# Reordering the weight differences and sums between the first and second group of a fused attention and maxout kernel

## The chip, the cores and the metric

The kernel runs on one core of one Trainium2 chip. The metric is the device time in microseconds. Of the kernel before, three runs gave 413.27 to 413.98 us, with a median of 413.74 us. In the profile, PE is the matrix engine (TensorE), DVE is VectorE, ACT is ScalarE, POOL is GpSimd, and SP is SyncE, which here issues nearly all transfers.

## The reference

Two blocks follow each other. The first is a gated linear attention, run over 768 tokens for 4 batches of 8 heads with a head dimension of 48:

```python
f = 1.0 / (1.0 + np.exp(-f_logit))
for t in range(S):
    state = f[:, :, t, :, None] * state + np.einsum('bhd,bhe->bhde', k[:, :, t], v[:, :, t])
    y[:, :, t] = np.einsum('bhd,bhde->bhe', q[:, :, t], state)
```

The result is laid out as 3072 tokens of 384 features and goes through a maxout layer. The three input weights are 384 x 768, the output weight is 768 x 384:

```python
h = np.maximum(np.maximum(x @ w1, x @ w2), x @ w3)
return (h @ w_out).astype(np.float32)
```

## The kernel before

The attention is cut into 24 units. A unit is a chunk of 64 tokens of two batches, all heads, so 128 rows. Four units make a group of 512 tokens, and the maxout layer runs on a group when its attention is complete. There are six groups, 0 to 5.

For a unit u, `sigmoids(u)` makes the gates on ScalarE and `scan(u)` their running products on VectorE. `after(u)` turns k on VectorE (L296, `kt`), multiplies it on GpSimd (L340, `kh`) and copies the ends (L339). `before(u)` makes the other running product (L347), turns q (L296, `qt`) and multiplies it on GpSimd (L351, `qh`). `carry(u)` scales the state (L357). On TensorE, `values`, `sums`, `pairs` and `finish` are the four blocks of 32 small products (L415, L433, L396, L504) that stand together once per unit. `keys_by_blocks` makes the transposes `ks` on VectorE (L382). ScalarE copies a finished unit into the token tile `xT` (L511), and two transfers (`pack`, L524) move parts of it to other partitions: one pair for the first three units of a group, and one pair for the last.

The maxout layer rewrites the maximum as differences: w2 and w3 have w1 subtracted, and the part with w1 becomes one linear product. Group 0 computes its maxima directly in `ffn_first`, while the weights arrive and are rounded. For the groups after it, `inputs_by_pairs` computes products of two token halves with fewer multiplications, in the manner of Strassen. It needs sums and differences of the weights, made once by `mix_in(0)` to `mix_in(3)` (L850): `w_sum[0]` for the step `fifth`, `w_sum[1]` for `sixth`, a difference written in place for `seventh` and `w_sum[2]` for `third`. The sums of tokens t1 to t5 come from `sums_of_x` (L865), and `join` (L899) adds two partial results; both are on GpSimd. The maxima are finished on VectorE (L924, L931, L932).

`outputs_by_pairs` multiplies the maxima by the output weights in the same manner, for all groups. It is a generator: each step issues some products (L629) and then yields its cost. Three PSUM banks a, b and c are in use. In group 0 its 24 steps, counted from 0, are:

- 0 to 7: plain products into b and a, after which ScalarE reads a (`read(a, 0)`, L634) and VectorE adds b (L637)
- 8 and 9: s1 into c, with a copy of c to `tops` on ScalarE (L683 or L685)
- 10 and 11: s2 into a, with `read(a, 1)`
- 12 to 15: products with the third difference and the linear part into a, with `read(a, 2)`, and then a sum of outputs on GpSimd (L697)
- 16 and 17: the linear part into c
- 18 and 19: products with the fourth difference into a, and the issue of the next group's `sums_of_x` when its tokens are there
- 20 and 21: the linear part with `lin_mix`, which is `w_mix[4]`, into a; a copy to the output on ScalarE (L714)
- 22 and 23: s4 into c, and a sum of outputs on VectorE

The flag `tight` puts s2 (steps 10 and 11) ahead of s1 (steps 8 and 9). Before the change it holds in the last two groups only.

The differences of output weights are made by `mix(0)` to `mix(4)` (L577); `mix(4)` writes `w_mix[4]`. In group 0, the list `made` says what is issued after which step: the sums of maxima s1 and s2 (L593) after steps 0 to 2, s4 after step 9, `mix_in(0)` to `mix_in(3)` after steps 10 to 13, and `mix(4)` after step 14. All these are on GpSimd.

The order is written out by hand. The main loop runs over the units u from 4 on (unit n = u + 1 is prepared while u is multiplied) and calls `fill(ns)` between its parts. `fill` draws steps from the pending maxout generators until their costs have used up a budget. Every engine works through its own queue in this order. SyncE's queue has, around unit 8, the moves of weights (`place`, L458 and L465), the pack transfers, and the loads of f, k and q (L183, eight transfers for a pair of units each) and v (L164). A load of q, or of k, for units 10 and 11 is issued in unit 8; those of units 12 and 13 in unit 9.

Of the kernel before, what the change touches and what calls it, by code (L numbers as in the profile page):

```python
# [55 lines left out]
def kernel(  # L56
# [12 lines left out]
    nc = tc.nc  # L69
    B, H, S, D = q.shape  # L70
    HP = H // 2
    NU = B // 2 * (S // C)
# [5 lines left out]
    GRP = 4  # L78
# [11 lines left out]
    def fast():  # L90
        ctx = ExitStack()
        with ctx:
# [511 lines left out]
            def outputs_by_pairs(g, hm, xT):  # L604
                tile_of = lambda p, n: slice((2 * p + n) * UT, (2 * p + n + 1) * UT)
                half = lambda n: slice(n * HD, (n + 1) * HD)
                mixed = g > 0
# [13 lines left out]
                    lin_mix = [w_mix[4][:, k] for k in range(NK)]  # L621
                    partial = [rests[:, 0], rests[:, 1], rests[:, 0]]
                last = g == NU // GRP - 1
                tight = g >= NU // GRP - 2
                begun = set()

                def into(b, p, lhs, rhs, part=slice(None)):
# [165 lines left out]
            def ffn_first(xT):  # L793
                hm = new_hm()
                steps = [(j, slice(n * HALF, (n + 1) * HALF)) for n in range(2) for j in range(J_HALF)]
                steps += [(j, slice(0, TOK)) for j in range(J_HALF, NJ)]
                n_step = 0
                for j, t in steps:
                    w = t.stop - t.start
                    for i in (1, 2):  # L800
                        p = yield from product(xT, j, i, t)
                        if i == 1:
                            nc.scalar.copy(hm[:, j, t], p)
                        else:
                            nc.vector.scalar_tensor_tensor(hm[:, j, t], hm[:, j, t], 0.0, p, op0=ALU.max, op1=ALU.max)
                        round_to(ROUNDED[n_step])
                        load_weights(2, rounded[0] - 1)
                        yield (1 if w == TOK else NK) * w * COLUMN
                        n_step += 1
                        if n_step in TURNED:  # L810
                            yield from turn(TURNED[n_step])
                for n in range(2 * NK + 2):
                    place(placed[0].bitcast(FP32), w_in[1], n)
                for a in range(NK):
                    for n, cost in enumerate(linear(a)):
                        round_to(rounded[0] + 1)
                        if a == 0 and n:
                            mix(n - 1)
                        if a == 0 and n == NK - 1:
                            mix(n)  # L820
                        yield cost
                for dst, src in ((placed[1].bitcast(FP32), w_in[2]), (w_lin, w_nat)):
                    for n in range(2 * NK + 2):
                        place(dst, src, n)
                mix(3)
                made = [[lambda jj=jj: sums_of_hm(hm, jj, slice(0, 2))] for jj in range(HJ)]
                made[-1] += [lambda jj=jj: sums_of_hm(hm, jj, slice(2, 3)) for jj in range(HJ)]
                made += [[], [], [], [], [], []]
                made += [[lambda jj=jj: sums_of_hm(hm, jj, slice(3, 4)) for jj in range(HJ)]]
                made += [[lambda n=n: mix_in(n)] for n in range(4)] + [[lambda: mix(4)]]  # L830
                made = iter(made)
                for cost in outputs_by_pairs(0, hm, xT):
                    for make in next(made, ()):
                        make()
                    yield cost
# [5 lines left out]
            w_two = [t.bitcast(FP32) for t in placed[0:2]]  # L841
            w_sum = [w_in[2][:, n] for n in range(NK)]

            def mix_in(n):

                dst, x, y, op = ((w_sum[0], w_two[1][:, 0], w_two[1][:, 1], ALU.add),
                                 (w_sum[1], w_sum[0], w_two[0][:, 0], ALU.subtract),
                                 (w_two[1][:, 0], w_two[0][:, 0], w_two[1][:, 0], ALU.subtract),
                                 (w_sum[2], w_two[0][:, 1], w_sum[1], ALU.subtract))[n]
                nc.gpsimd.tensor_tensor(dst, x, y, op=op)  # L850

            packed, summed = {}, {}
            halves = lambda xT, k, h: xT[:, k, h * HALF:(h + 1) * HALF]
# [15 lines left out]
            def inputs_by_pairs(g, hm, xT):  # L869
                X = lambda k, h: halves(xT, k, h)  # L870
                t1, t2, t3, t4, t5 = sums_of_x(g)
                s1, s2, s4 = w_sum
                s3 = w_two[1][:, 0]
                COST = 2 * HALF * COLUMN
                out = lambda n, h: hm[:, 2 * n:2 * n + 2, h * HALF:(h + 1) * HALF]
                first, u3 = rests[:, 0:2, 0:HALF], tops[:, 2:4, 0:HALF]
                A, B, U5 = {}, {}, {}

                def into(b, n, w, x, begin=False):
                    for j in range(2):  # L880
                        nc.tensor.matmul(b[:, j * HALF:(j + 1) * HALF], lhsT=w[:, (2 * n + j) * 128:(2 * n + j + 1) * 128],  # L881
                                         rhs=x, start=begin and j == 0, stop=True, skip_group_check=True)

                def plain(n):
                    B[n] = bank(True)
                    into(B[n], n, w_two[0][:, 1], X(1, 0), True)
                    yield COST
                    into(B[n], n, w_two[0][:, 2], X(2, 0))
                    nc.scalar.copy(out(n, 0), two(B[n]))  # L889
                    yield COST  # L890

                def start(n):
                    A[n] = bank()
                    into(A[n], n, w_two[0][:, 0], X(0, 0), True)
                    nc.scalar.copy(first, two(A[n]))
                    yield COST

                def join(n):
                    nc.gpsimd.tensor_tensor(out(n, 0), out(n, 0), first, op=ALU.add)  # L899

                def fifth(n):
                    into(B[n], n, s1, t1, True)
                    U5[n] = two(new_top(TOK))
                    nc.scalar.copy(U5[n], two(B[n]))
                    yield COST

                def sixth(n):
                    into(A[n], n, s2, t2)
                    nc.scalar.copy(out(n, 1), two(A[n]))
                    yield COST  # L910

                def seventh(n):
                    into(A[n], n, s3, t3)
                    yield COST
                    into(A[n], n, w_two[1][:, 2], X(2, 1))
                    nc.scalar.copy(u3, two(A[n]))
                    nc.gpsimd.tensor_tensor(u3, u3, U5[n], op=ALU.add)
                    yield COST

                def third(n):  # L920
                    into(B[n], n, s4, X(1, 1))
                    yield COST
                    into(B[n], n, w_two[0][:, 2], X(2, 1))
                    nc.vector.tensor_tensor(out(n, 1), two(B[n]), out(n, 1), op=ALU.add)  # L924
                    yield COST

                def fourth(n):
                    into(A[n], n, w_two[1][:, 1], t4)
                    yield COST
                    into(A[n], n, w_two[1][:, 2], t5)  # L930
                    nc.vector.scalar_tensor_tensor(out(n, 0), out(n, 0), 0.0, two(A[n]), op0=ALU.max, op1=ALU.max)  # L931
                    nc.vector.scalar_tensor_tensor(out(n, 1), out(n, 1), 0.0, u3, op0=ALU.max, op1=ALU.max)  # L932
                    sums_of_hm(hm, n)
                    if g == 1:
                        for i in ((0, 1), (2, 3, 4), ())[n]:
                            mix_x(i)
                    yield COST

                yield from start(0)
                yield from plain(0)  # L940
                join(0)
                if g > 1:
                    store_late()
                yield from plain(1)
                yield from sixth(0)
                yield from fifth(0)
                for n in range(1, NJ // 2):
                    if n > 1:
                        yield from plain(n)
                    yield from seventh(n - 1)  # L950
                    yield from start(n)
                    join(n)
                    yield from third(n - 1)
                    yield from fifth(n)
                    yield from sixth(n)
                    yield from fourth(n - 1)
                    store_late()
                yield from seventh(NJ // 2 - 1)
                yield from third(NJ // 2 - 1)
                yield from fourth(NJ // 2 - 1)  # L960
# [35 lines left out]
            with tc.manual_schedule():  # L996
# [78 lines left out]
                for u in range(GRP, NU):  # L1075
                    n = u + 1
# [38 lines left out]
                    if n < NU:  # L1115
                        after(n)
                        before(n)
                    check_range(u - CHECKS, 0)
                    fill(part)
                    if BY_ROWS < u + 2 < NU and u % GRP == 0:  # L1120
# [292 lines left out]
```

## Time and profile before

| what | value |
|---|---|
| median of three runs | 413.74 us (413.27 to 413.98) |
| the profiled execution | 414.71 us |
| its span in the profile | 413.0 us |
| mean granted TensorE clock | 0.992 |
| TensorE busy (products) | 392.8 us, 95% |
| VectorE busy | 296.5 us, 72% |
| GpSimd busy | 257.5 us, 62% |
| ScalarE busy | 181.3 us, 44% |
| bytes moved by transfers | 47.21 MB |

Times in the views are microseconds from the start of the span. A row of a timeline gives the start, the duration, the engine, the line, the operation, the tiles written and read with their shape, and how many instructions are merged. In brackets stands the idle time before it and what ended it. A row of the waits names who waited for whom, the total, the number of times and the longest.

### The profile page before, as it was taken

The page shows a single profiled execution, that of the slowest core. Times are in us where ns is not written, and L with a number is a line of the kernel's source. Part 1 is how long each engine was busy: PE and PEld are TensorE (multiplying, and loading weights), DVE is VectorE, ACT ScalarE, POOL GpSimd, SP SyncE. Part 2 cuts the span into 40 slices and gives each one's busy share as a digit, 9 for nine tenths or more (in the row PEclk, how much of TensorE's full clock was granted, in tenths as well). Part 3 has the DMA queues.
Part 4 walks back from the last instruction along what each step waited for, and adds up shares of the span by engine and source line. Part 5 has one row for each costly group of instructions (what it writes and reads, how often), then busy time and mean ns, then how long its engine had stood idle before and what let it go on. Part 6 is the DMA issues. An engine that isn't in the chain of part 4 may idle for free.

```text
span 413.0 us, 11671 instructions
## 1 busy us (share of the span) xinstructions
PE 392.8 (95%) x4658; PEld 341.9 (83%) x4658; DVE 296.5 (72%) x571; ACT 181.3 (44%) x431; POOL 257.5 (62%) x284
## 2 busy tenths in 40 slices
PE   4988999999959999999999999999999999999995
PEld 3766765559858889998889998889988889988995
DVE  5997797999947799899799898898985650001600
ACT  2477787423204352335442435442344424487220
POOL 2179595789994777747685487496287860435700
PEclk9999999999969999999999999999999999999999
DMA  8988986768356775367664277645374002452002
GB/s 165 238 250 223 307 234 80 155 88 138 87 95 89 109 151 112 80 85 111 97 155 73 59 116 95 115 116 104 50 141 124 2 17 83 115 153 76 2 19 62
DMA packets 181594, 47.21 MB, mean 114 GB/s; under 512 B 160480, under 2 KB 179232, under 8 KB 181536
## 3 DMA queue, kind: packets, MB, share of 16 engines
q1 hardware_dynamic: 178048, 45.62, 54.0%
q10 hardware_dynamic: 3488, 0.81, 0.9%
q8 instruction: 37, 0.61, 0.6%
q14 instruction: 21, 0.17, 0.1%
HBM read 37.75 MB, written 4.72 MB: 103 GB/s over the span
## 4 chain that ended last, share of the span: by engine, by line
PE 79%; SPq 7%; POOL 5%; DMA 2%; DVE 2%; issue 2%; ACT 2%; POOLq 0%
PE p L881 19%; PE p L629 16%; PE tr L881 15%; PE tr L629 12%; PE p L542 6%; PE y L415 3%; SPq L183 3%; PE a L396 2%; SPq L174 2%; PE y L504 2%; PE a L433 2%; DMA raw<-in_moe_w_dram 2%; POOL w_in L850 1%; SPq L164 1%; POOL w_in L752 1%
## 5 line engine op out<-in xcount | busy, mean ns | idle before, releaser
L382 DVE STREAM_TRANSPOSE ks<-kh 32x128 f32<-32x128 f32 x256 | 77.4, 302 | 14.9 <-POOL kh L340 10.7
L881 PE MATMUL tr<-xT,placed 128*128 128x256 f32 x180 | 44.4, 384 | 0.0
L339 POOL COPY ends<-r 128x8 f32<-128x8 f32 x24 | 7.9, 328 | 50.0 <-DVE r L329 50.0
L329 DVE TENSOR_TENSOR_SCAN r<-gate,from_one 128x520 f32<-128x520 f32 x24 | 33.2, 1384 | 6.4 <-issue 3.0
L881 PEld LDWEIGHTS tr<-xT,placed 128*128 128x128 f32 x180 | 33.5, 190 | 4.9
L340 POOL TENSOR_TENSOR kh<-kt,r 128x512 f32<-128x512 f32 x18 | 31.9, 1771 | 8.5 <-DVE kt L296 8.5
L542 PE MATMUL p<-xT,w_in 128*128 128x256 f32 (+1 forms) x108 | 33.9, 458 | 3.3 <-POOL w_in L752 2.2
L593 POOL TENSOR_TENSOR w_in<-hm 128x256 f32<-128x256 f32 x18 | 13.3, 739 | 33.5 <-DVE hm L932 33.5
L511 ACT COPY xT<-y 64x256 f32<-64x256 f32 (+1 forms) x60 | 22.1, 369 | 22.7 <-PE y L504 22.0
L347 DVE TENSOR_TENSOR_SCAN prod<-gate,from_inv 128x520 f32<-128x520 f32 x24 | 31.6, 1317 | 0.0
L881 PE MATMUL tr<-xT,w_in 128*128 128x256 f32 x120 | 30.8, 379 | 0.0
L629 PE MATMUL p<-placed,hm 128*128 128x192 f32 x144 | 29.8, 333 | 0.7 <-POOL kh L340 0.7
L881 PE MATMUL p<-w_in,placed 128*128 128x256 f32 x120 | 30.4, 382 | 0.0
L637 DVE TENSOR_TENSOR o<-tr,w_in 128x384 f32<-128x384 f32 (+1 forms) x11 | 5.7, 521 | 33.4 <-PE tr L629 29.0
L542 PEld LDWEIGHTS p<-xT,w_in 128*128 128x128 f32 x108 | 19.5, 190 | 12.3 <-issue 6.0
L881 PE MATMUL p<-xT,placed 128*128 128x256 f32 x120 | 29.2, 379 | 0.0
L629 PE MATMUL tr<-w_out,w_in 128*128 128x192 f32 x144 | 29.0, 329 | 0.0
L924 DVE TENSOR_TENSOR hm<-tr,hm 128x512 f32<-128x512 f32 x15 | 10.2, 683 | 23.1 <-PE tr L881 16.2
L258 POOL TENSOR_TENSOR w_in<-top_bits,rest_bits 128x384 uint32<-128x384 uint32 x18 | 21.4, 1197 | 7.6 <-DVE top_bits L252 4.7
L881 PEld LDWEIGHTS p<-w_in,placed 128*128 128x128 f32 x120 | 22.4, 190 | 4.4 <-issue 1.6
L629 PEld LDWEIGHTS p<-placed,hm 128*128 128x128 f32 x144 | 23.8, 190 | 2.3 <-ACT w_in L634 1.1
L899 POOL TENSOR_TENSOR hm<-hm,rest_bits 128x512 f32<-128x512 f32 x15 | 19.1, 1272 | 10.2 <-ACT hm L889 10.2
(168 smaller groups left out, 989.9 us busy)
## 6 DMA issues: line engine op xcount, KB each, us to landing
raw<-in_moe_w_dram SPq DMA_DIRECT2D x24, 384.0 KB, 4.4
v_ld<-in_v_dram SPq DMA_DIRECT2D x48, 96.0 KB, 3.3
placed<-in_moe_w_dram SPq DMA_DIRECT2D x12, 384.0 KB, 5.9
out_dram<-o SPq DMA_DIRECT2D x45, 96.0 KB, 2.2
placed<-in_moe_w_out_dram SPq DMA_DIRECT2D x6, 384.0 KB, 6.2
f_ld<-in_f_logit_dram SPq DMA_DIRECT2D x36, 64.0 KB, 2.7
k_ld<-in_k_dram SPq DMA_DIRECT2D x36, 64.0 KB, 2.6
q_ld<-in_q_dram SPq DMA_DIRECT2D x36, 64.0 KB, 2.8
```

The source lines that it names most:

```text
L183: nc.sync.dma_start(out=blocks[nm][u // 2 % 2][p0:p0 + 32, n, :, 0:w], in_=src[:, par::2, t0 + n * 32:t0 + (n + 1) * 32, e0:e0 + w].rearrange(
L258: nc.gpsimd.tensor_tensor(dst, by(top), by(rest), op=ALU.add)
L329: nc.vector.tensor_tensor_scan(r[:, 0:LEN][:, ::-1], flat(gate)[:, ::-1], flat(from_one)[:, ::-1], 1.0, op0=ALU.mult, op1=ALU.max)
L340: (nc.vector if u < BY_ROWS else nc.gpsimd).tensor_tensor(kh.rearrange("p h a t -> p a h t"), kt, by_batch(r[:, 1:LEN + 1].rearrange("p (x ...
L347: nc.vector.tensor_tensor_scan(flat(prod), flat(gate_tiles[u % 2]), flat(from_inv[u % 2]), 1.0, op0=ALU.mult, op1=ALU.max)
L382: nc.vector.transpose(ks[n * 32:(n + 1) * 32, :, par, e0:e0 + 32], kh[p0:p0 + 32, :, a, t0:t0 + 32])
L511: nc.scalar.copy(xT[o, :, t0 + a * C:t0 + (a + 1) * C], y[i, a, 0:HP * C].rearrange("p (h t) -> p h t", h=HP))
L542: nc.tensor.matmul(p if w < TOK else p.rearrange("p (two t) -> p two t", two=2), lhsT=w_in[i][:, kt, j * 128:(j + 1) * 128], rhs=x[:, t.st ...
L593: engine.tensor_tensor(dst, x, y, op=op)
L629: nc.tensor.matmul(b[:, p * HD:(p + 1) * HD], lhsT=x, rhs=w, start=id(b) not in begun, stop=True, skip_group_check=True)
L881: nc.tensor.matmul(b[:, j * HALF:(j + 1) * HALF], lhsT=w[:, (2 * n + j) * 128:(2 * n + j + 1) * 128], rhs=x, start=begin and j == 0, stop= ...
L899: nc.gpsimd.tensor_tensor(out(n, 0), out(n, 0), first, op=ALU.add)
```

## The change

In group 0, the flag `tight` now holds as well, so the s2 products come ahead of the s1 products. `mix(4)` is issued after step 10, and `mix_in(0)` and `mix_in(1)` after steps 11 and 12. `mix_in(2)` moves to VectorE, behind `before(9)` in unit 8 of the main loop. `mix_in(3)` stays on GpSimd and is issued at the beginning of the second group's input products, behind its `sums_of_x`.

```diff
-                tight = g >= NU // GRP - 2
+                tight = not mixed or g >= NU // GRP - 2
...
                 made += [[lambda jj=jj: sums_of_hm(hm, jj, slice(3, 4)) for jj in range(HJ)]]
-                made += [[lambda n=n: mix_in(n)] for n in range(4)] + [[lambda: mix(4)]]
+                made += [[lambda: mix(4)]] + [[lambda n=n: mix_in(n)] for n in range(2)]
                 made = iter(made)
...
-            def mix_in(n):
+            def mix_in(n, engine=nc.gpsimd):
 
                 dst, x, y, op = ((w_sum[0], w_two[1][:, 0], w_two[1][:, 1], ALU.add),
                                  (w_sum[1], w_sum[0], w_two[0][:, 0], ALU.subtract),
                                  (w_two[1][:, 0], w_two[0][:, 0], w_two[1][:, 0], ALU.subtract),
                                  (w_sum[2], w_two[0][:, 1], w_sum[1], ALU.subtract))[n]
-                nc.gpsimd.tensor_tensor(dst, x, y, op=op)
+                engine.tensor_tensor(dst, x, y, op=op)
...
+                if g == 1:
+                    mix_in(3)
                 yield from start(0)
                 yield from plain(0)
                 join(0)
...
                     if n < NU:
                         after(n)
                         before(n)
+                    if u == 2 * GRP:
+                        mix_in(2, nc.vector)
                     check_range(u - CHECKS, 0)
                     fill(part)
```

## The prediction

> **What bounds the kernel now.** I read the chain that ended last first: after 126 us it is almost wholly TensorE, and before that it runs through GpSimd's weight differences at L850 and L577. So I asked which waits TensorE has between 90 and 126 us (us in total, times, longest):
>
> ```profile
> PE p L629 <- POOL placed L577: 4.2, 1, 4.2
> PE p L629 <- POOL kh L340: 0.7, 1, 0.7
> ```
>
> The timelines of GpSimd and of TensorE (start, us, engine, line) show the first wait from both sides.
>
> ```profile
> 106.67 2.11 POOL L593 TENSOR_TENSOR w_in<-hm,w_in 128x256 f32<-128x256 f32 x3
> 108.73 1.82 POOL L850 TENSOR_TENSOR w_in<-placed 128x768 f32<-128x768 f32 x1
> 110.63 1.82 POOL L850 TENSOR_TENSOR w_in<-w_in,placed 128x768 f32<-128x768 f32 x1
> 112.41 2.75 POOL L850 TENSOR_TENSOR placed<-placed,placed 128x768 f32<-128x768 f32 x1
> 115.12 2.73 POOL L850 TENSOR_TENSOR w_in<-placed,w_in 128x768 f32<-128x768 f32 x1
> 117.82 1.39 POOL L577 TENSOR_TENSOR placed<-w_in 128x576 f32<-128x576 f32 x1
> ```
>
> ```profile
> 112.95 2.11 PE L629 MATMUL p<-placed,hm 128*128 128x192 f32 x12
> 119.26 4.21 PE L629 MATMUL p<-placed,xT 128*128 128x192 f32 x12 [4.20 <-POOL placed L577]
> 123.26 2.46 PE L629 MATMUL tr<-w_out,w_in 128*128 128x192 f32 x12
> ```
>
> Four mix_in sums (9.1 us) stand in GpSimd's queue ahead of mix(4), which TensorE needs next. It idles 4.20 us, and then 24 matmuls take from 119.26 to 125.72 where 24 at the usual pace (1.95 per 12, start to start) take 3.9. The view by windows has a granted clock of 0.65 from 119.3 to 126.0 and 1.00 on both sides. The price is 4.2 + 2.6 us.
>
> SyncE decides what becomes of it. From 84 to 149 us it issues transfers back to back:
>
> ```profile
> 119.43 1.30 SPq L524 DMA_DIRECT2D xT<-xT  x2
> 122.28 4.29 SPq L183 DMA_DIRECT2D k_ld<-in_k_dram  x8
> 126.70 5.14 SPq L183 DMA_DIRECT2D q_ld<-in_q_dram  x8
> 132.42 4.83 SPq L183 DMA_DIRECT2D f_ld<-in_f_logit_dram  x8
> 137.35 5.26 SPq L183 DMA_DIRECT2D k_ld<-in_k_dram  x8
> ```
>
> The last q transfer (issued 131.42) took this to land, by the view of that tile:
>
> ```profile
> DMA to landing us min/median/max: 3.1/3.1/3.1
> ```
>
> So q of units 10 and 11 is there at 134.5. VectorE turns it at 135.86, only 1.3 us later, and then works almost without a break until TensorE needs its maxima (VectorE, then TensorE):
>
> ```profile
> 135.86 0.68 DVE L296 STREAM_TRANSPOSE qt<-q_ld 128x512 f32<-128x512 f32 x1
> 164.57 0.69 DVE L932 SCALAR_TENSOR_TENSOR hm<-hm,top_bits 128x512 f32<-128x512 f32 x1
> ```
>
> ```profile
> 165.30 0.81 PE L629 MATMUL p<-w_out,hm 128*128 128x192 f32 x4
> ```
>
> **The Trainium skill.** "TensorE: Matmul & The Clock Gate", What's actually happening, says that an idle window of about 3.4 us halves the array's clock and that a similar busy time restores it. The trace agrees: 4.20 us of idling cost 2.6 us more, the 0.7 us wait nothing. "SBUF — State Buffer", Who interferes with whom, says that GpSimd and VectorE exclude each other on a shared port pair when VectorE has two SBUF inputs and GpSimd reads SBUF. The trace agrees in kind: a 128x768 sum took 1.82 us, and 2.75 beside VectorE's scans. The end of a transfer I take from the trace, 2.4 to 3.1 us.
>
> **The change, part by part.**
>
> mix(4) behind the s4 sums, ahead of mix_in: it starts at 108.73 and takes 1.39, so it is done at 110.1. TensorE reaches step 20 (lin_mix) at 115.06 by the rows above. The wait goes, and with it the slow clock: 4.2 + 2.6 = 6.8 us.
>
> s2 ahead of s1 (`tight`): the 0.66 us wait at 104.82 was for read(a, 1) on ScalarE (104.20 + 0.48). The s1 products now stand between, so it goes. In exchange s2 needs read(a, 0), which ended at 100.18; TensorE wanted to go on at 100.10 and starts at about 100.3. Net gain 0.4. Together 7.2: TensorE begins group 1 at 118.4 instead of 125.56. Its first products need only the first copy into xT (L524, issued 111.51 to 113.56), not the second (landed about 122.2).
>
> mix_in(0) and (1) follow mix(4): 110.1 to 112.0 and to 113.8, or 114.7 beside the scan. Then the output sum (1.0), ends, kh(9), qh(9) at about 118.5, state at 119.3. kh(9) came at 120.26 before, so this is no delay. The five x sums wait for the second copy, 122.3 to 126.0, where they started at 123.3 before.
>
> mix_in(3) behind them on GpSimd: 1.82 to 2.75, done by 127.8 to 128.8. third(0) is the eleventh step of group 1: 118.4 + 10 x 0.865 (a step of four 128x256 rows, 2.59 for three in the chain) + 2.1 of attention between (127.3 to 129.4) = 129.2. Hidden with 0.4 us to spare. join(0) behind it ends at 129.2 to 130; its next reader on ScalarE (L895) wants it at 136.74 - 7.2 = 129.5. If the cover is gone, up to 1 us of TensorE.
>
> mix_in(2) on VectorE: not seen there at this size. The nearest row, 128x384 at L752, took 0.55 to 1.36; twice that is 1.1 to 2.7, and I take 1.1. It stands behind qt(9), which ended at 116.86, where VectorE idled 4.62 us for kh(9). Queued behind it are the transposes of kh(9), which may now start at 117.3 and start at 118. TensorE needs them a unit later. Cost nothing; without cover 1.1 to 2.7. It issues no transfer, and no SyncE instruction moves.
>
> **Where the 7.2 us stop.** SyncE's order and pace don't hang on TensorE here: its queue is full from 84 us. So q(10) still lands at 134.5, but TensorE would come to pairs(10) at 142.73 - 7.2 = 135.5. VectorE turns q from 134.57 to 135.25, GpSimd's qh takes 1.18, so pairs(10) starts at 136.5: 1.0 us of a new wait. Worse, VectorE stood waiting for q with its other work queued behind. From qt(10) to the end of L932 in the third pair it took 165.26 - 135.86 = 29.4 us, of which it idled 0.42 + 0.28 + 1.48 + 0.34 = 2.5. Compressed, with 0.2 given back to a sum on GpSimd at L917, that is 27.1 us: 134.57 + 27.1 = 161.7. TensorE's second half of the 165.30 group (at 165.62) then starts at 161.7, and its gain is 3.9 us. It waits some 2 us there, too short to slow the clock. Behind it the sums at L593 and qh(12) move 3.6 us with VectorE (qh(12) at 168.6, pairs(12) at 169.0), so no more is lost. From 175 on SyncE waits for TensorE again (its xT copies), and the rest moves as one.
>
> Sum against the profiled execution: span 413.0 - 3.9 = 409.1; device time 414.71 - 3.9 = 410.8. That execution stands 0.97 above the median 413.74, so I predict 413.74 - 3.9 = 409.8.
>
> **Rivals.**
>
> Loads don't bind, all is kept: 413.74 - 7.2 = 406.5. For: one of q's issues took 1.36 us where its neighbours took 0.49, so the landing may come 0.9 sooner. Against: it would have to come 3.3 us sooner, at 131.2, when SyncE is still issuing it. Chance 0.13.
>
> The new 2 us wait at 159 to 161.7 slows the clock as the old one did: 3.9 - 2.6 = 1.3, so 412.4. For: it falls together with short waits for the first half of the maxima. Against: 0.7 us did not, and 2 is under the stated window. Chance 0.08.
>
> Slower: the compressed VectorE stretch from 134.6 collides with GpSimd more often. Each collision costs about 0.9 us (2.03 against 1.18 for kh at L340; 2.75 against 1.82 at L850). It decides from five more on: 3.9 - 5 x 0.9 = -0.6; six give 415.2. For: nearly every VectorE operation there has two inputs. Against: the order on both queues is the same, and both move together. Chance 0.06.
>
> No change: mix(4) waits for something else. Its inputs, the linear products, were copied out at 92.5, and what it overwrites was free before; or the q loads fall 3 us further behind. 413.7, chance 0.05.
>
> **How the numbers follow.** The forecast has 0.68, with a range of its own of 408.6 to 411.0: 0.9 sooner for q's landing, 1.2 later for a collision and mix_in(3) coming late. 407.0 to 412.6 holds it, the clock case and the edge of the full gain, about 8 in 10. 0.2% (0.8 us) is about what a measurement of this kernel can tell from no change. Faster 0.68 + 0.13 + 0.08 = 0.89, same 0.05, slower 0.06.
>
> **What would show it.** Right: no wait of lin_mix's products for L577, clock 1.00 from 115 to 126, group 1's first products at 118 to 119, a wait of VectorE before qt(10) ending at 134 to 135, waits of TensorE at pairs(10) (about 1 us) and at the last hm rows of group 1 (about 2), and the shift constant from 170 on. Wrong: q landing sooner with TensorE unbroken, or TensorE waiting for L850 at third(0), or a clock below 1 after 130.

## The result and the profile after

The changed kernel takes 408.62 us (median of 4 runs, 406.68 to 410.12), the kernel before 413.50 us beside it. The ratio is 0.9878, with a 95% interval of 0.9833 to 0.9923: 4.9 us faster, between 3.2 and 6.9. The forecast was 409.8.

The profiled execution took 408.11 us, with a span of 406.4 us. The page has a granted clock of 9 tenths or more in all forty slices; before, one slice had 6. The same stretch of TensorE's timeline as before (start, us, engine, line) now reads:

```profile
111.04 2.11 PE L629 MATMUL p<-placed,hm 128*128 128x192 f32 x12
112.99 2.12 PE L629 MATMUL p<-placed,xT 128*128 128x192 f32 x12
114.94 2.11 PE L629 MATMUL tr<-w_out,w_in 128*128 128x192 f32 x12
116.89 1.03 PE L881 MATMUL p<-xT,placed 128*128 128x256 f32 x4
```

Steps 18 to 23 of group 0 follow each other without a gap, at 1.95 us per twelve. GpSimd has mix(4) ahead of two sums, and the third sum is on VectorE:

```profile
107.46 1.42 POOL L577 TENSOR_TENSOR placed<-w_in 128x576 f32<-128x576 f32 x1
108.82 1.82 POOL L850 TENSOR_TENSOR w_in<-placed 128x768 f32<-128x768 f32 x1
110.73 2.72 POOL L850 TENSOR_TENSOR w_in<-w_in,placed 128x768 f32<-128x768 f32 x1
```

```profile
115.08 1.10 DVE L850 TENSOR_TENSOR placed<-placed,placed 128x768 f32<-128x768 f32 x1
130.16 0.71 DVE L296 STREAM_TRANSPOSE qt<-q_ld 128x512 f32<-128x512 f32 x1 [0.95 <-DMA q_ld<-in_q_dram]
```

The second row is the turn of q(10). VectorE now waits for the load, 0.95 us, which it did not do before. It comes late with the maxima, and TensorE waits for them once:

```profile
157.41 1.19 PE L629 MATMUL p<-w_out,hm 128*128 128x192 f32 x4 [0.61 <-DVE hm L931]
```

Where the time went is seen from the block of 32 small products at L415, which TensorE runs once per unit. These are its starts in the two timelines:

| L415 block | before | after | difference |
|---|---|---|---|
| unit 6 | 93.11 | 91.85 | -1.3 |
| unit 7 | 105.97 | 104.06 | -1.9 |
| unit 8 | 127.38 | 118.71 | -8.7 |
| unit 9 | 141.76 | 133.10 | -8.7 |
| unit 10 | 156.91 | 148.25 | -8.7 |
| unit 11 | 171.89 | 164.38 | -7.5 |
| span | 413.0 | 406.4 | -6.6 |

The first 1.3 us are no effect of the change: up to there both kernels run the same instructions, and the two executions differ. Then 0.65 us come from the order of the products and 6.76 us from the wait and its slow clock, 7.4 us in all. Some 1.15 us are given back between units 10 and 11, of which the wait shown is 0.61. From unit 11 on the difference stays at 7.5 us up to the last product. The last 0.9 us are in the final stores: 4.2 us from the last product to the end of the span before, 5.1 us after. They are no effect of the change either, because the second profile of the changed kernel has 4.2 again. So this pair of profiles puts the change at 7.4 - 1.15 = 6.3 us, more than the 4.9 us of the medians: the profiled execution of the kernel before was slower than its median, that of the changed kernel faster.

### The profile page after: what moved, and what is told of

Same layout as the page of the kernel before. It is cut to its first block, busy times and chain, and to the rows that moved or that the text cites. A ratio compares the mean times of both kernels' runs of the same rounds, so it can differ in the third digit from the quotient of the medians.

```text
span 406.4 us, 11673 instructions
## 1 busy us (share of the span) xinstructions
PE 390.6 (96%) x4658; PEld 339.5 (84%) x4658; DVE 298.4 (73%) x572; ACT 181.1 (45%) x431; POOL 256.4 (63%) x283
## 4 chain that ended last, share of the span: by engine, by line
PE 83%; DVE 6%; SPq 3%; POOL 3%; DMA 2%; issue 1%; ACT 1%; POOLq 0%
PE p L629 18%; PE p L881 17%; PE tr L881 15%; PE tr L629 13%; PE p L542 7%; PE y L415 3%; PE p L783 3%; PE a L396 2%; PE y L504 2%; PE a L433 2%; SPq L174 2%; DMA raw<-in_moe_w_dram 2%; DVE ks L382 1%; POOL w_in L258 1%; SPq L164 1%
## 5 line engine op out<-in xcount | busy, mean ns | idle before, releaser
L339 POOL COPY ends<-r 128x8 f32<-128x8 f32 x24 | 8.6, 357 | 48.7 <-DVE r L329 48.7
L881 PEld LDWEIGHTS tr<-xT,placed 128*128 128x128 f32 x180 | 33.6, 190 | 4.8
L340 POOL TENSOR_TENSOR kh<-kt,r 128x512 f32<-128x512 f32 x18 | 31.9, 1772 | 8.5 <-DVE kt L296 8.5
L634 ACT COPY w_in<-p 128x384 f32<-128x384 f32 x15 | 7.2, 479 | 41.8 <-PE p L629 41.8
L280 ACT ACTIVATE raw<-top_bits 128x384 f32<-128x384 f32 x48 | 25.2, 526 | 0.4
```

What stands on the lines that cost most here:

```text
L280: nc.scalar.activation(over, size, AF.Relu, scale=(-1 / HI_MIN, 1.0)[step - 1], bias=(1.0, -HI_END * (1 - 2.0 ** -24))[step - 1], accum_ou ...
L340: (nc.vector if u < BY_ROWS else nc.gpsimd).tensor_tensor(kh.rearrange("p h a t -> p a h t"), kt, by_batch(r[:, 1:LEN + 1].rearrange("p (x ...
```

## The experiments

Each is the median of 4 to 22 runs, beside the kernel before on the same chip, and the ratio is to that kernel; gains in us are worked out from the ratio. The kernel before had medians of 413.37, 413.81 and 412.65 us beside the three sets of four below. Each kernel also left one profile. Differences between blocks of TensorE are those of that profile. The trace has two records for each product of this kernel, and the counts of products below are counts of records, as in the views, save where the text says otherwise.

**The order of the products alone.**

```diff
 # kernel before
-                tight = g >= NU // GRP - 2
+                tight = not mixed or g >= NU // GRP - 2
```

> The kernel before with s2 ahead of s1 in group 0 and nothing else. Theory of the forecast (GpSimd's queue sets TensorE's start at step 20, whatever TensorE does before): the 0.7 us wait at read(a, 1) goes, TensorE reaches step 20 some 0.6 us sooner and waits 4.8 instead of 4.2 us for mix(4); the time stays within 0.3 us of before. Rival (the order of the products carries a part of the gain by itself): 0.5 us or more faster than before.

Measured: 412.97 us, ratio 0.9999 (0.9984 to 1.0014). The waits of TensorE between 90 and 200 us (us in total, times, longest) are a single row:

```profile
PE p L629 <- POOL placed L577: 4.8, 1, 4.8
```

The wait of 0.7 us is gone and the one behind it has grown by the same amount. Step 20 starts 26.15 us after the block of unit 6 in both profiles, so GpSimd's queue set its start.

**mix(4) first, all four sums still on GpSimd in group 0.**

```diff
 # kernel before
-                made += [[lambda n=n: mix_in(n)] for n in range(4)] + [[lambda: mix(4)]]
+                made += [[lambda: mix(4)]] + [[lambda n=n: mix_in(n)] for n in range(4)]
```

> The kernel before with mix(4) ahead of all four mix_in sums, which stay on GpSimd in group 0; s1 stays ahead of s2. Theory of the forecast (the wait for mix(4) and the slow clock behind it are the gain): no wait before step 20, clock 1.00, and 4 to 6 us faster than before, as the whole change. A new wait of 1 to 1.5 us at pairs(9) for qh(9), which now comes behind the four sums, and is covered by the later waits for loads. Rival (moving the two sums is what gives the gain, GpSimd is the bound around unit 9): less than half of the gain of the whole change, under 2.5 us.

Measured: 410.90 us, ratio 0.9928 (0.9903 to 0.9954), 3.0 us faster: less than the 4 to 6 us of the theory, more than the 2.5 us of the rival. The block of unit 8 is 7.3 us earlier than before's, and that of unit 7 was 0.5 us earlier, so 6.8 us were gained there, as expected. The block of unit 9 is only 3.5 us earlier. TensorE's timeline shows where the rest went:

```profile
122.13 0.69 PE L396 MATMUL a<-qh,kh 48*64 48x64 f32 x32 [0.86 <-POOL qh L351]
123.60 0.71 PE L504 MATMUL y<-qh,state 48*48 48x64 f32 x32 [0.78 <-ACT seen L422]
124.25 4.45 PE L881 MATMUL tr<-xT,placed 128*128 128x256 f32 x12
```

The wait for qh(9) was foreseen. The second was not. ScalarE's copy at L895 waits for GpSimd until 122.92, and the small copy at L422, which TensorE needs, stands behind it in ScalarE's queue. And the twelve products behind both waits take 4.28 us to the next start instead of 2.6. The view by windows (length, busy time and count of TensorE, its weight loads, VectorE, ScalarE and GpSimd, then the granted clock, the transfers' share and GB/s) gives the reason:

```profile
121.00:126.00 5.00, 3.36 (x88) 2.70 (x81) 4.77 (x15) 1.73 (x5) 4.92 (x7) 0.81 0.61 85
```

Two waits of 0.8 us close together, with small products around them, brought the clock down for some microseconds: 1.6 us of waiting and 1.7 us of slow products. These make 3.3 of the 3.7 us that are gone at unit 9. So moving sums out of GpSimd's way does have a worth of its own, at unit 9, and not at the wait that the profile of before shows.

**q of units 10 and 11 loaded twice, in both kernels.**

```diff
 # in each of the two kernels
                     if BY_ROWS < u + 2 < NU and u % GRP == 0:
                         load(u + 2, one, "q")
+                        if u == 2 * GRP:
+                            load(u + 2, one, "q")
```

> The kernel before with the q of units 10 and 11 loaded twice, so that SyncE's queue is eight transfers (about 4.2 us) longer there and the second q lands that much later. Theory of the loads (forecast): before, the load has slack, 1.3 us at VectorE's turn of q, 2.3 us of VectorE's idle time behind it and 0.4 us at TensorE: 0 to 0.7 us slower. Rival (the loads are not near the bound at all): no change here and none in the changed kernel with the same load doubled.

> The changed kernel with the q of units 10 and 11 loaded twice, eight transfers (about 4.2 us) more in SyncE's queue. Theory of the loads: the slack is used up by the gain of TensorE, so VectorE waits about 4 us longer before it turns q(10), TensorE waits 3 to 4 us more at the last hm rows of group 1, and the kernel is 3 to 4.5 us slower than the changed one, near 412. Rival (loads hidden): within 0.5 us of the changed kernel.

Measured on the kernel before: 414.28 us, ratio 1.0019 (1.0002 to 1.0036), 0.8 us slower (0.1 to 1.5), where 0 to 0.7 was expected. On the changed kernel: 413.68 us, ratio 1.0011 (0.9992 to 1.0030); the changed kernel itself was at 0.9878, and at 0.9913 in a later set, so the same load costs it 4 to 5.5 us, all that it had gained, as far as these runs can tell. The waits of VectorE, first before and then changed, have these rows:

```profile
DVE qt L296 <- DMA q_ld<-in_q_dram: 3.0, 1, 3.0
```

```profile
DVE qt L296 <- DMA q_ld<-in_q_dram: 7.4, 1, 7.4
```

In the kernel before, a wait of 3.0 us at q(10) is more than half absorbed: TensorE's block of unit 11 moves by 1.3 us against the one before it. In the changed kernel TensorE waits at pairs(10), and hardly at the maxima (0.2 us), where the wait was expected:

```profile
PE a L396 <- POOL qh L351: 4.5, 1, 4.5
```

The clock was 0.50 from 136.6, within this wait, to 143.4, so 6.9 us were lost up to unit 10, and 0.8 more up to unit 11. The slack of the load is what the change used up.

**The changed kernel once more.**

> The changed kernel once more, beside the others on one chip. Theory of the loads: what is left of the 7.2 us depends on when q(10) lands, so the gain is 4 to 6 us and the runs lie 3 us or more apart, where those of before lie within 2. Rival (all is kept): 7 us faster, runs no farther apart than before's.

Measured: 410.44 us (408.19 to 411.41), ratio 0.9913 (0.9882 to 0.9943), 3.6 us faster. The gain lies a little under the expected range. The expectation on the spread was wrong for the kernel before, whose 30 runs in this set lie between 412.28 and 415.76 themselves. Part of that spread goes with the clock: of the 76 runs of the kernel before in the three sets, the 22 with a mean clock of 0.990 or less have a median of 413.95 us, the 25 with 0.995 or more one of 412.90. In this profile VectorE waits longer for q:

```profile
131.06 0.71 DVE L296 STREAM_TRANSPOSE qt<-q_ld 128x512 f32<-128x512 f32 x1 [1.95 <-DMA q_ld<-in_q_dram]
```

TensorE then loses 2.4 us between units 10 and 11, instead of 1.15 in the first profile. It waits 0.7 us for the maxima, and 1.0 us at L504 for ScalarE, which itself waited 5.4 us for VectorE's L932. One microsecond more of waiting for q goes with 1.3 us more lost.

**The moves of the linear weights issued later.** These ten transfers on SyncE stand ahead of the copies of xT and of the loads for units 10 and 11, and their result is needed late in group 1.

```diff
 # changed kernel
-                for dst, src in ((placed[1].bitcast(FP32), w_in[2]), (w_lin, w_nat)):
-                    for n in range(2 * NK + 2):
-                        place(dst, src, n)
+                for n in range(2 * NK + 2):
+                    place(placed[1].bitcast(FP32), w_in[2], n)
...
                     if BY_ROWS < u + 2 < NU and u % GRP == 0:
                         load(u + 2, one, "q")
+                        if u == 2 * GRP:
+                            for i in range(2 * NK + 2):
+                                place(w_lin, w_nat, i)
```

> The changed kernel with the ten moves of the linear weights (L458 and L465 into w_lin, needed only late in group 1) issued behind q(10) in unit 8 rather than ahead of the first xT copy. Nothing is left out. Theory of the loads: k and q of units 10 and 11 land some 6 us sooner, VectorE does not wait at qt(10), TensorE waits neither at pairs(10) nor at the last hm rows of group 1, the clock stays at 1.00, and the kernel is 7 us faster than before (near 406.3), 1.5 to 2.5 us faster than the changed one, with runs closer together. Rival (the loads do not bind the changed kernel, VectorE's own work or GpSimd's does): within 0.5 us of the changed kernel.

Measured: 406.90 us (406.30 to 407.56), ratio 0.9829 (0.9804 to 0.9854): 7.1 us faster than before and 3.5 us faster than the changed kernel beside it, more than the 1.5 to 2.5 us expected. SyncE's timeline has the loads of k and q some 7 us sooner than in the changed kernel, where q's began at 123.72:

```profile
111.80 4.29 SPq L183 DMA_DIRECT2D k_ld<-in_k_dram  x8
116.19 4.16 SPq L183 DMA_DIRECT2D q_ld<-in_q_dram  x8
120.39 2.05 SPq L458 DMA_DIRECT2D w_in<-w_in  x2
```

VectorE turns q with no wait ahead of it (the row below), and TensorE's waits between 90 and 200 us are an empty list.

```profile
129.15 0.68 DVE L296 STREAM_TRANSPOSE qt<-q_ld 128x512 f32<-128x512 f32 x1
```

Two things stay open. The copies of xT and the loads of f and v move forward with those of k and q, and what each is worth by itself was not tried; the doubled load ties the effect to q, because it leaves the copies of xT where they are. And of the 3.5 us, the profiles show only 0.8 (against the first profile of the changed kernel) and 2.1 (against the second) up to unit 11. Within these limits, SyncE's queue of loads bound the changed kernel, and this version beats both.

**The same late moves in the kernel before.** The diff is the one above, on the kernel before.

> The kernel before with the same ten moves issued behind q(10). Theory of the forecast: GpSimd's queue sets TensorE's start at step 20, the loads have slack: within 0.5 us of before. Rival (SyncE's queue costs time in any case): 1 us or more faster than before.

Measured: 413.94 us, ratio 1.0009 (0.9994 to 1.0024). TensorE waits 4.2 us for L577 as before. Sooner loads are worth nothing while GpSimd's queue sets the pace: the second repair gains only where the first is made.

**Work in the wait of the kernel before.**

```diff
 # kernel before, ahead of step 20
+                if not mixed:
+                    busy(9)
                 into(a, 0, X(1), lin_mix)
```

> The kernel before with nine 128x256 products more (of constants, their result unused) ahead of step 20 of group 0, about 3.9 us of work for TensorE inside its wait for mix(4). Theory (the wait has two prices, 4.2 us of idling and 2.6 us of slow clock behind it): the start of step 20 does not move, the clock stays at 1.00, steps 20 to 23 take 3.9 instead of 6.5 us; 2 to 2.6 us faster than before. Rival (what is slow behind the wait is not the clock but the weights or the late sums): no change or slower.

Measured: 411.39 us, ratio 0.9938 (0.9917 to 0.9958), 2.6 us faster (1.7 to 3.4) for nine products more, which are 18 records. TensorE's timeline:

```profile
114.01 4.05 PE L985 MATMUL p<-from_one,ident 128*128 128x256 f32 x18
118.37 2.22 PE L629 MATMUL p<-placed,xT 128*128 128x192 f32 x12 [0.30 <-POOL placed L577]
120.42 2.11 PE L629 MATMUL tr<-w_out,w_in 128*128 128x192 f32 x12
```

Step 20 starts where it did (0.9 us sooner, as all of this execution is), and the 24 products behind it take 4.0 us to the start of group 1 instead of 6.3 (119.26 to 125.56). That is the clock's price by itself, 2.3 us in these profiles.

This price is not set by the length of the wait alone. The same 24 products took 6.7 us with the doubled load and 5.7 us in the kernel before with late moves, behind waits of 4.2 us, and 5.7 us behind the 4.8 us with the order alone, where 3.9 is usual: 1.8 to 2.8 us. The views by windows of the kernel before and of the one with the order alone show why:

```profile
117.10:124.00 6.90, 4.74 (x15) 4.74 (x16) 1.20 (x4) 0.49 (x2) 6.90 (x8) 0.51 0.62 98
118.10:121.60 3.50, 3.46 (x11) 3.46 (x12) 1.20 (x4) 0.00 (x0) 3.50 (x5) 0.51 0.48 91
```

Just outside of these windows the clock is 1.00. In the first, 6.8 us at half the clock begin 2.1 us before step 20, so 4.7 us of them fall on work and cost half of that, 2.4 us. In the second, 3.4 us begin with step 20 and cost 1.7.

**Parts of the change undone, with the loads out of the way.** Four versions have the late moves. The first undoes the order of the products:

```diff
 # version with late moves
-                tight = not mixed or g >= NU // GRP - 2
+                tight = g >= NU // GRP - 2
```

> The version with the late moves of the linear weights, with s1 ahead of s2 in group 0 again (that part of the change undone). Theory: with nothing behind it that takes the gain back, the 0.7 us wait at read(a, 1) returns and reaches the end: 0.5 to 0.8 us slower than the version with late moves. Rival (the order of the products is worth nothing anywhere): the same within 0.2 us.

Measured: 407.44 us, ratio 0.9856 (0.9832 to 0.9880). This is 1.1 us slower than the version with late moves by the ratios, but the two intervals overlap, so the times do not decide. The profiles show the place: against the block of unit 6, TensorE is 0.64 us later at units 7 to 10, and 0.27 at unit 11. The version with late moves loses 0.4 us between units 10 and 11, though the list names no wait, and this one nothing. That this is TensorE catching up with VectorE's maxima is likely, but not shown. The second puts mix(4) behind the two sums that stay:

```diff
 # version with late moves
-                made += [[lambda: mix(4)]] + [[lambda n=n: mix_in(n)] for n in range(2)]
+                made += [[lambda n=n: mix_in(n)] for n in range(2)] + [[lambda: mix(4)]]
```

> The version with the late moves, with mix(4) behind mix_in(0) and (1), which stay in group 0; mix_in(2) and (3) stay moved. Theory: mix(4) ends at about 113.4 and TensorE comes to step 20 at 113.0, so 0.4 to 0.6 us of waiting and no slow clock: within 0.7 us of the version with late moves; taking two sums out of the way does the work that putting mix(4) first does. Rival (mix(4) has to be first): 2 us or more slower.

Measured: 407.07 us, ratio 0.9852 (0.9828 to 0.9877), with this wait of TensorE and no other from 90 to 200 us:

```profile
PE p L629 <- POOL placed L577: 0.4, 1, 0.4
```

By the ratios it is about 1 us slower than the version with late moves, with intervals that overlap; by the blocks, 0.6 at unit 8 and 0.25 at unit 11. With two sums out of the way, mix(4) need not be first: in the profile its later place costs well under the rival's 2 us. The third has mix_in(2) at its new place, but on GpSimd:

```diff
 # version with late moves
-                        mix_in(2, nc.vector)
+                        mix_in(2)
```

> The version with the late moves, with mix_in(2) at its new place but on GpSimd. Theory: it delays the x sums by 1.8 us to 122.6 for t2, where sixth(0) needs it at about 123.4, and mix_in(3) to 126.6, where third(0) needs it at 127.8: within 0.3 us of the version with late moves. Rival (GpSimd has no room around unit 9, the move to VectorE is needed): 1 us or more slower, with TensorE waiting at sixth(0), third(0) or for the copies of ScalarE behind join(0).

Measured: 406.32 us, ratio 0.9838 (0.9818 to 0.9858). GpSimd's timeline has both sums, and TensorE waits nowhere from 90 to 200 us:

```profile
118.69 1.83 POOL L849 TENSOR_TENSOR placed<-placed,placed 128x768 f32<-128x768 f32 x1
124.83 1.83 POOL L849 TENSOR_TENSOR w_in<-placed,w_in 128x768 f32<-128x768 f32 x1
```

What counts for mix_in(2) is the later place; the engine makes no difference that these runs can tell. The fourth is the kernel with mix(4) first and four sums on GpSimd, with late moves:

```diff
 # kernel with mix(4) first; the late moves as above
-                for dst, src in ((placed[1].bitcast(FP32), w_in[2]), (w_lin, w_nat)):
...
+                                place(w_lin, w_nat, i)
```

> The kernel before with mix(4) ahead of four mix_in sums on GpSimd and with the late moves of the linear weights; s1 ahead of s2. Theory: the loads were not what held the kernel with mix(4) first alone back; GpSimd was. The waits for qh(9) (0.9 us) and for ScalarE's copy behind the output sum (0.8 us), and the slow clock behind them (1.7 us), stay: within 0.7 us of that kernel (about 3 us faster than before), 3 to 4 us slower than the version with late moves. Rival (the loads held it): within 1.5 us of the version with late moves.

Measured: 409.28 us, ratio 0.9906 (0.9885 to 0.9928), 3.9 us faster than before, against 3.0 without the late moves, with intervals that overlap. In both profiles the block of unit 9 stands 45.6 us behind that of unit 6. The waits of 0.9 and 0.8 us and the clock of 0.81 from 121 to 130 us are all there. In its profile TensorE loses 3.7 us between the blocks of units 8 and 9 against the version with late moves. For that kernel GpSimd's queue was the bound, not the loads.

## Why the prediction was right

The time lies 1.2 us under the forecast and in its range; the second set, with 3.6 us of gain, brackets the forecast of 3.9 from the other side. That the forecast comes so near is in part luck. It takes back 3.3 of the 7.2 us at q(10), from the queue of one execution, and this loss changes from execution to execution: 1.15 and 2.4 us in the two profiles, 2.5 and 3.8 if the gains of the two sets are set against the 7.4 of the profile.

The wait and the clock: forecast 6.8 us, 6.76 in the profile. The split was off by a little: 2.6 sets the end of the last of 24 products against a pace from start to start. From start to start they took 6.30 us against 3.90, which makes 2.4 for the clock and 4.36 for the wait. The work put into the wait says 2.3 in the profile and 2.6 (1.7 to 3.4) in the time. In other executions this term can be 1.8 to 2.8. mix(4) had to be ready by 115.06 and was, by far.

The order of the products: forecast 0.4, measured 0.65 at its place. At the end it is worth nothing in the kernel before. With the loads out of the way, 0.27 us of it are left at unit 11, and the times do not resolve it.

mix_in(2) on VectorE: 1.10 us, as taken from twice the L752 row, and hidden as said. The new places on GpSimd: state was forecast to end at 119.3 and did, but by luck. This execution was 1.3 us ahead, so in its own time the forecast was 118.0. The sum of outputs took 1.95 us where 1.0 was said, and L339 took 0.92, where its row before had 0.20. No wait of TensorE came of it.

mix_in(3): the margin at third(0), 0.4 us, was put too small by far. The second copy of xT landed before 119.26, so the x sums did not wait for it. mix_in(3) ended at 124.64 where 127.8 to 128.8 was said, and third(0) began at 127.83, so the margin was 3.2 us.

The loads: the mechanism was right. VectorE waits before qt(10), comes late with L932 of the third pair, and TensorE waits there. The stretch from qt(10) to the end of L932 took 27.8 us (130.16 to 157.95) where 27.1 was said. The term that was mis-sized is the landing of q, in the step "so q(10) still lands at 134.5". It landed about 130.1: 1.3 us sooner because this whole execution was ahead, and 3.1 us sooner because SyncE was further on in its queue (some 2.5, half of them from before 88 us) and the last transfer landed faster (some 0.6). So the wait of TensorE at pairs(10), forecast at 1.0 us, was not there, and the one at the maxima was 0.6 us, not 2. The idea that this queue's pace could be carried over from one execution to the next was the weak step. In the eight profiles in which the moves stand ahead of them, the q loads begin 31.9 to 33.8 us after the block of unit 6: 33.6 in the one that the prediction read, 31.9, the earliest, in this one. With the load doubled, the wait at pairs(10) is there, at 4.5 us.

The rival of all kept, 406.5, is what the changed kernel reaches once the loads are moved: 406.9. The rival of the slow clock did not happen in the profiles of the changed kernel, but the argument against it, that 0.7 us did not slow the clock and 2 us are too short, does not hold in general. In the kernel before the clock had fallen after 2.1 us of idling already, and in the kernel with mix(4) first after two waits of 0.8. Of the longer rows that the rival of collisions between VectorE and GpSimd expects, a few were seen (1.95 instead of 1.00 us for the sum of outputs, 1.30 instead of 0.68 for L932 of the first pair), but nothing that makes the kernel slower than before.

Not shown is which microseconds separate the longer executions of the changed kernel from the profiled ones; both of its profiles are from the shorter half. That q lands later in the longer ones is argued from the two profiles and the doubled load. The slow clock does not explain it: the three executions of the second set above 411 us had mean clocks of 0.998, 0.995 and 0.998. A clock of 0.998 is worth 0.8 us, and two of these three are 2.8 us and more above the fastest, at 408.19.

## What to carry to other kernels

A wait that is removed gives its engine's time back only as far as the next resource keeps up: ask of each load that was just in time before how much later it is now, relative to the engine that got faster. Take that landing from more than one profile. Look for transfers in front of it in the issuing queue that nobody needs soon; moving ten of them was worth 3.5 us here, and nothing while the first bound stood. Count the clock into the price of a wait, with a range (1.8 to 2.8 us behind waits of 4.2 to 4.8 us here), and count short waits that lie close together as one.

## What the runs showed of the hardware

Two idle stretches of 0.86 and 0.78 us with 32 small products (48 rows by 64 columns) between them were enough for a granted clock of 0.81 over 121 to 130 us in the kernel with mix(4) first. A single one of 0.6 to 0.7 us never was, nor were one of 0.99 and one of 0.69 us with 7 us between them, in the second profile of the changed kernel. Wherever the clock fell between 90 and 200 us, it stood at 0.50 for about 3.4 us (four profiles) or 6.8 us (three). 0.81 over these 9 us is 3.4 us at 0.50, and half of 3.4 is the 1.7 us that the products lost. "TensorE: Matmul & The Clock Gate", What's actually happening, in the Trainium skill speaks of an idle window of about 3.4 us; here the clock fell after less. In the kernel before it fell 2.1 us after TensorE's products had ended (115.06 to 117.1). With mix(4) first the sum of the idle time in 3 us was 1.6, so light work seems to count as little. That the small products are the reason was not tried.

An issue on SyncE mostly took 0.49 to 0.65 us, but now and then 1.0 to 1.9, at other places in each execution: 1.87 at 107.00 us in the profile before, where the same transfer took 0.59 after, and 1.58 at 120.96 after, where it took 0.49 before. Transfers issued just ahead of such a stretch landed together, after up to 4.4 us. Several of these make some microseconds of difference between two executions of the same queue. Their cause is open.
